# Sums over four tokens on VectorE or on TensorE, in the attention stage of a three-stage kernel

## The chip, the core and the metric

The kernel runs on one core of a Trainium2 chip. The metric is the device time of one execution in microseconds, as the median of three runs.

## The reference

Three layers follow each other. The first is attention over 4 batches, 8 heads, 576 tokens of 64 numbers, in two branches that are added: a coarse one, in which queries, keys and values are averaged over each four neighbouring tokens (144 positions), and a local one, in which each token sees the tokens less than four places away. The second is a layer of 8 experts with one expert a token, of which a linear score switches tokens off. The third is a gated layer of width 1536. Only the averages of queries and keys matter for the change.

```python
    q_d = q.reshape(B, H, Sd, factor, D).mean(axis=3)
    k_d = k.reshape(B, H, Sd, factor, D).mean(axis=3)
    v_d = v.reshape(B, H, Sd, factor, D).mean(axis=3)
    out_d = sm_attn(q_d, k_d, v_d)
    out_up = np.repeat(out_d, factor, axis=2)
...
    attn = attn / (np.sum(attn, axis=-1, keepdims=True) + 1e-09)
    out_local = np.matmul(attn, v)
    return (out_up + out_local).astype(np.float32)
```

## The kernel before

**The attention stage.** Queries and keys come in 12 units u of 192 tokens, three to a batch, and in each unit there are two loads n (0 queries, 1 keys) of 128 partitions (two heads of 64) by 4 head pairs by 192 tokens, in float32 (step `lq`, line 494, tile `qk`, five buffers). Float32 values are worked on as two float16 halves: ScalarE writes the high half (step `ph`, helper `hi_`, line 340) and VectorE subtracts it from the value for the low half (`pl`, helper `lo_`, line 343), both into the tile `qks` of the batch, of which there are two. The local branch (18 tiles i of 128 tokens: `ls` scores on TensorE, `lm` maximum and subtraction on VectorE, `le` exponential, `lt` and `lc` turn, `lV` values, `lr` and `ln` division) reads `qks`. The sums over four tokens (`pp`, line 511) are 16 products a unit: the float16 unit matrix times every fourth column of the halves, four columns and two halves accumulated in one PSUM bank for each of queries and keys (tile `qkd`). These sums are split into halves again, into the tile `qkh` (`qh` on ScalarE, `ql` on VectorE), and the coarse branch of a batch reads that (`ds` scores, line 548; `dm`, `dq`, `de`, `dt`, `dc`, `dv`, `dr`, `dn`) and writes its result to memory (`do`, tile `od`), from where each local tile loads its part (`lu`) and adds it (`xa`). GpSimd adds the coarse values of four tokens (`svd`, lines 539 and 540). The router follows (`gp`, `gd`, `gr`, `gk`), with GpSimd writing rows out by index.

**The order.** All steps of this stage are entered in a list with their engine, an estimated duration, the steps that they need, and the buffers that they take and release. A planner, class `Plan`, runs them through a model once, as the kernel is built: of the steps that are ready it takes the one that can start first, and of those the one with the least key, which is the length of the path behind it (negative) plus a correction from the table `PRI`. The instructions are then issued in that order on each engine's own in-order queue, and loads on SP's. Where the model sees TensorE without work for over 0.1 us, or with too few columns lately, it puts in filler products of zeros (line 411, 0.108 us in the model). Costs in the model: `pp` 1.6 us a unit on TensorE, `pl` 0.95, `ql` 0.54, `ls` 1.65, `lm` 1.7. The table `PRI` has 63 entries, one for each kind of step.

**After it** come the experts (first product at line 1060, in `h_first`), whose weights are loaded as buffers of the attention stage come free, and the gated layer.

## Time and profile before

| | us |
|---|---|
| median of 3 runs (747.73 to 748.56) | 748.16 |
| the profiled execution | 746.42 |
| its span, first to last instruction | 744.6 |
| TensorE / VectorE / ScalarE / GpSimd busy in the span | 704.0 / 498.7 / 386.7 / 282.6 |

The profiled execution is a single one; its span is the time from the first to the last instruction that the profiler recorded, and the rest of its time lies around that. Products are pipelined and their ends are modelled, so two that overlap count once in a busy time.

### The profile page before, as it was taken

The numbers are of one execution on the slowest core, as the hardware profiler recorded it, in microseconds if no ns is written. First come the engines' busy times: TensorE is split into PE (matmuls) and PEld (weight loads), VectorE is DVE, ScalarE is ACT, GpSimd is POOL, SyncE is SP. The second block draws the span as 40 slices with busy tenths as digits, with TensorE's granted clock in tenths as the row PEclk, the third lists the DMA queues.
The fourth block names the chain that finished last, engine by engine and source line by source line (L and its number), as shares of the span: only waits on it lengthen the run. The fifth ranks groups of instructions, "written<-read, shape, count | busy, mean of one in ns | idle before, by whom it ended". The sixth has DMA issues, their size and how long they took to land.

```text
span 744.6 us, 16389 instructions
## 1 busy us (share of the span) xinstructions
PE 704.0 (95%) x6567; PEld 466.7 (63%) x6567; DVE 498.7 (67%) x940; ACT 386.7 (52%) x766; POOL 282.6 (38%) x261
## 2 busy tenths in 40 slices
PE   8889788889899999989999899999999999999997
PEld 6677677778777888766665554455666666544443
DVE  6677587777688788769888989976668886300000
ACT  6565475452577776647777752445555655300000
POOL 5345575354100000236886775234434454200000
PEclk9999899999999999999999999999999999999999
DMA  8889887571799999865766511840000000001001
GB/s 258 246 267 273 190 208 197 149 176 50 230 353 341 346 364 284 269 218 183 217 179 187 155 27 42 163 92 1 2 0 1 1 1 1 1 28 43 29 29 42
DMA packets 95334, 108.82 MB, mean 146 GB/s; under 512 B 51248, under 2 KB 68658, under 8 KB 94679
## 3 DMA queue, kind: packets, MB, share of 16 engines
q1 hardware_dynamic: 91319, 99.80, 46.5%
q0 software_dynamic: 2880, 6.89, 2.9%
q10 hardware_dynamic: 1056, 1.05, 0.5%
q8 instruction: 52, 0.85, 0.5%
q14 instruction: 27, 0.22, 0.1%
HBM read 81.69 MB, written 17.30 MB: 133 GB/s over the span
## 4 chain that ended last, share of the span: by engine, by line
PE 42%; DVE 9%; ACT 3%; issue 3%; POOL 0%; ACTq 0%; DVEq 0%; POOLq 0%
PE p L1430 19%; PE op L1513 19%; PE gvp L1257 3%; DVE cb L1167 2%; DVE stg L1166 2%; DVE sg L1270 1%; DVE yg L1213 1%; DVE xphl L346 1%; ACT u L340 1%; ACT stg L1159 1%; ACT sg L1265 0%; DVE xpT L346 0%; ACT stg L1160 0%; PE xpp L1221 0%; ACT xpT L340 0%
## 5 line engine op out<-in xcount | busy, mean ns | idle before, releaser
L1513 PE MATMUL op<-w,u 128*128 128x512 f16 x648 | 140.2, 379 | 0.0
L1257 PE MATMUL gvp<-xpT,w 128*128 128x384 f16 (+1 forms) x720 | 111.1, 315 | 4.5 <-ACT sg L1265 2.2
L1513 PEld LDWEIGHTS <-u 128*128 128x128 f16 x648 | 63.5, 98 | 76.2
L1257 PEld LDWEIGHTS <-w 128*128 128x128 f16 x720 | 67.6, 98 | 47.2 <-issue 5.5
L343 DVE SCALAR_TENSOR_TENSOR w<-stg,w 128x1024 f16<-128x1024 f32 x64 | 79.7, 1273 | 17.9 <-ACT w L340 17.8
L346 POOL TENSOR_TENSOR w<-cb,w 128x512 f16<-128x512 f32 x36 | 52.2, 1450 | 83.6 <-ACT w L340 83.6
L1430 PEld LDWEIGHTS <-w 128*128 128x128 f16 x528 | 51.6, 98 | 36.1 <-issue 2.1
L340 ACT ACTIVATE w<-stg 128x1024 f16<-128x1024 f32 x64 | 65.7, 1051 | 16.0 <-DMA stg<-in_moe_w 14.6
L1048 PEld LDWEIGHTS <-w 128*128 128x128 f16 x672 | 55.7, 98 | 1.7
L1048 PE MATMUL hp<-xe,w 128*128 128x192 f16 x672 | 56.6, 246 | 0.0
L340 ACT ACTIVATE y<-op 128x512 f32<-128x512 f32 x18 | 10.7, 592 | 84.9 <-PE op L1513 84.4
L1430 PE MATMUL p<-t,w 128*128 128x384 f16 x244 | 50.1, 326 | 1.6 <-DVE sc L1303 1.6
L1430 PE MATMUL p<-xpT,w 128*128 128x384 f16 x264 | 46.5, 326 | 0.0
L1167 DVE SCALAR_TENSOR_TENSOR cb<-stg 128x512 int32<-128x512 int32 x36 | 42.1, 1171 | 3.5
L1430 PE MATMUL p<-t,s7h 128*128 128x384 f16 x176 | 42.9, 326 | 1.1 <-ACT sa L1454 1.1
L1083 PE MATMUL ya<-w,hT 128*128 128x512 f16 (+1 forms) x216 | 42.9, 356 | 0.0
L346 POOL TENSOR_TENSOR u<-sa,u 128x384 f16<-128x384 f32 x22 | 20.1, 915 | 49.9 <-ACT u L340 49.9
L1430 PEld LDWEIGHTS <-s7h 128*128 128x128 f16 x264 | 25.8, 98 | 18.3 <-issue 1.3
L511 PE MATMUL qkd<-qks,identh 128*128 128x192 f16 x192 | 34.7, 350 | 2.0 <-issue 2.0
L539 POOL TENSOR_TENSOR vr<-vr 72x1024 f32<-72x1024 f32 x8 | 18.8, 2356 | 41.7 <-DMA vr<-in_vr 38.4
L411 PE MATMUL wbank<-wz 128*128 128x252 bf16 x209 | 30.9, 287 | 2.5 <-POOL wz L407 1.3
L1083 PEld LDWEIGHTS <-hT 128*128 128x128 f16 x216 | 20.5, 98 | 20.3 <-issue 1.6
(196 smaller groups left out, 1389.8 us busy)
## 6 DMA issues: line engine op xcount, KB each, us to landing
stg<-in_moe_w SPq DMA_DIRECT2D x64, 512.0 KB
qk<-in_qk SPq DMA_DIRECT2D x24, 384.0 KB
stg<-in_moe_w_out SPq DMA_DIRECT2D x12, 512.0 KB
stg<-in_moe_w_gate SPq DMA_DIRECT2D x11, 512.0 KB
stg<-in_moe_w_val SPq DMA_DIRECT2D x11, 512.0 KB
vw<-in_vw SPq DMA_DIRECT2D x18, 284.4 KB
vr<-in_vr SPq DMA_DIRECT2D x8, 576.0 KB
up<-outd SPq DMA_DIRECT2D x18, 256.0 KB
```

The source lines that it names most:

```text
L340: act.activation(out=o, in_=i, func=func, scale=s)
L343: dve.scalar_tensor_tensor(out=o, in0=i, scalar=s, in1=h, op0=op, op1=ALU.subtract)
L346: eng.tensor_tensor(out=o, in0=i, in1=h, op=ALU.subtract)
L411: pe.matmul(out=wbank[:, 260:512], lhsT=wz[:, 0:128], rhs=wz[:, 0:252], start=True, stop=True)
L511: pe.matmul(out=p[:, n], lhsT=identh, rhs=qk_at(u, n, m // 4).rearrange("p b (g r) -> p b g r", r=4)[:, :, :, m % 4], start=(m == 0), stop ...
L539: pool.tensor_tensor(out=r[:, 0:2], in0=r[:, 0:2], in1=r[:, 2:4], op=ALU.add)
L1048: pe.matmul(out=p, lhsT=wt[e, kk][:, wl, m * 128:(m + 1) * 128], rhs=xe[e][:, xl + kk, :], start=(n == 0), stop=(n == 11))
L1083: pe.matmul(out=p, lhsT=hT[e][:, hl, m, 0:128], rhs=w[:, o:o + n], **f)
L1167: dve.scalar_tensor_tensor(out=b, in0=hi_w, scalar=3, in1=lo_w, op0=ALU.logical_shift_left, op1=ALU.bitwise_or)
L1257: pe.matmul(out=pp[n][:, o:o + width], lhsT=w[:, wl, n, kk * 128:(kk + 1) * 128], rhs=xpT[blk][:, xl + kk, o:o + width], start=(j == 0), s ...
L1430: pe.matmul(out=p, lhsT=l(wl)[:, 128 * kk:128 * kk + 128], rhs=rr(xl, kk), start=first and j == 0, stop=last and j == 5, skip_group_check= ...
L1513: pe.matmul(out=p, lhsT=u[:, ul, t * 128:(t + 1) * 128], rhs=w[:, wl, f % 2, :], start=(n == 0), stop=(n == 3 * NF - 1))
```

## The change

The sums are made by VectorE, by one reduction for each loaded tile (two a unit), straight from the float32 tile `qk` into a float32 tile `qkd` in SBUF, of which there are two. The step `pp` thereby becomes two steps, `("pp", u, 0)` and `("pp", u, 1)`, on VectorE's queue at 0.88 us each in the plan; they need the load alone and release the loaded tile, which now has three readers. The tile `qks` loses three readers a batch, and the sums take no PSUM bank. Since the float32 values are not scaled yet, the splitting of the sums (`qh`, `ql`) scales them. The planner's key gets a second correction, for a single step, and the table `PRI` has 904 entries, 841 of them for single steps, with other values for the kinds too. The entry of `pp` in the table of columns that count for TensorE's fillers goes. The two tables are cut here.

```diff
--- before.py
+++ after.py
@@ -53,7 +53,7 @@
 C_IO = C_MASK + 4 * W
 C_N = C_IO + CAP
 
-PRI = {'cs': -192.4, 'ct': 204.9, 'dc': -158.3, 'de': 83.2, 'dm': -115.1,
...
+PRI = {'cs': 29.0, 'ct': 151.8, 'dc': 13.5, 'de': 89.5, 'dm': -179.4,
...
+        ('pp', 5, 0): 58.5, ('pp', 5, 1): 16.6, ('lv', 5): -22.6, ('lm', 7): -20.2, ('lt', 8, 0): -41.4,
...
 
 
 def constants():
@@ -136,7 +136,7 @@
             return t
 
         kind = lambda n: n[0] if isinstance(n, tuple) else n
-        key = {n: (ops[n][6] + self.pri.get(kind(n), 0.0) - length(n), m) for m, n in enumerate(ops)}
+        key = {n: (ops[n][6] + self.pri.get(kind(n), 0.0) + (self.pri.get(n, 0.0) if isinstance(n, tuple) else 0.0) - length(n), m) for m, n in enumerate(ops)}
         ready = [n for n in ops if not nneed[n]]
         base = {n: 0.0 for n in ready}
         order, when, busy, lock = [], {}, [], {}
@@ -504,12 +504,10 @@
                     qks[b] = a2.tile([128, 2, 2, 4, S], F16, tag="qks", name="qks")
                 hi_(qk_at(u, n, 0), qk[u, n], SQ)
 
-            def prep_p(u):
-                p = qkd[u] = bank([128, 2, 4, 48], "qkd")
-                for n in range(2):
-                    for m in range(8):
-                        pe.matmul(out=p[:, n], lhsT=identh, rhs=qk_at(u, n, m // 4).rearrange("p b (g r) -> p b g r", r=4)[:, :, :, m % 4],
-                                  start=(m == 0), stop=(m == 7), skip_group_check=True)
+            def prep_p(u, n):
+                if n == 0:
+                    qkd[u] = a2.tile([128, 2, 4, 48], F32, tag="qkd", name="qkd")
+                dve.tensor_reduce(out=qkd[u][:, n].rearrange("p b (g o) -> p b g o", o=1), in_=qk[u, n].rearrange("p b (g r) -> p b g r", r=4), axis=AX.X, op=ALU.add)
 
             def prep_l(u, n):
                 lo_(qk_at(u, n, 1), qk[u, n], qk_at(u, n, 0), SQ)
@@ -521,10 +519,10 @@
             def pool_h(u):
                 if u // 3 not in qkh:
                     qkh[u // 3] = a2.tile([128, 2, 2, 4, S // 4], F16, tag="qkh", name="qkh")
-                hi_(qkh_at(u, 0), qkd[u], 1.0)
+                hi_(qkh_at(u, 0), qkd[u], SQ)
 
             def pool_l(u):
-                lo_(qkh_at(u, 1), qkd[u], qkh_at(u, 0), 1.0)
+                lo_(qkh_at(u, 1), qkd[u], qkh_at(u, 0), SQ)
 
 
             vr, dS, dP, dTp, dT, dO, dR, od = {}, {}, {}, {}, {}, {}, {}, {}
@@ -863,7 +861,7 @@
                 scat.append(d.ins)
 
 
-            pl = Plan({"bank": 7, "fb": 1, "qk": NQK, "qks": 2, "qkh": 2, "vw": NV, "vr": 1, "vd": 2, "dP": 2, "dT": 2,
+            pl = Plan({"qkd": 2, "bank": 7, "fb": 1, "qk": NQK, "qks": 2, "qkh": 2, "vw": NV, "vr": 1, "vd": 2, "dP": 2, "dT": 2,
                        "od": 1, "lP": 2, "lT": 3, "xhl": 6, "up": 2, "xT": 2, "stg": NST, "lr": 3, "dr": 3}, PRI)
             DL = 2.0
             tiles_of = {b: [i for i in range(NTILE) if b in ((2 * i) // 9, (2 * i + 1) // 9)] for b in range(B)}
@@ -882,14 +880,15 @@
                 for n in range(2):
                     z = (u, n)
                     first = u % 3 == 0 and n == 0
-                    pl.add(("lq",) + z, "SP", 1.2, lambda z=z: load_qk(*z), take=[("qk", ("qk",) + z, 2)], late=DL)
+                    pl.add(("lq",) + z, "SP", 1.2, lambda z=z: load_qk(*z), take=[("qk", ("qk",) + z, 3)], late=DL)
                     pl.add(("ph",) + z, "ACT", 0.82, lambda z=z: prep_h(*z), need=[("lq",) + z] + ([] if first else [("ph", 3 * b, 0)]), rel=[("qk",) + z],
-                           take=[("qks", ("qks", b), len(tiles_of[b]) + 3)] if first else [])
+                           take=[("qks", ("qks", b), len(tiles_of[b]))] if first else [])
                     pl.add(("pl",) + z, "DVE", 0.95, lambda z=z: prep_l(*z), need=[("ph",) + z], rel=[("qk",) + z])
-                pl.add(("pp", u), "PE", 1.6, lambda u=u: prep_p(u), need=["ih", ("pl", u, 0), ("pl", u, 1)], take=[("bank", ("pb", u), 1)], rel=[("qks", b)])
-                pl.add(("qh", u), "ACT", 0.49, lambda u=u: pool_h(u), need=[("pp", u)] + ([("qh", 3 * b)] if u % 3 else []),
+                for n in range(2):
+                    pl.add(("pp", u, n), "DVE", 0.88, lambda u=u, n=n: prep_p(u, n), need=[("lq", u, n)] + ([("pp", u, 0)] if n else []), take=[] if n else [("qkd", ("qkd", u), 1)], rel=[("qk", u, n)])
+                pl.add(("qh", u), "ACT", 0.49, lambda u=u: pool_h(u), need=[("pp", u, 1)] + ([("qh", 3 * b)] if u % 3 else []),
                        take=[] if u % 3 else [("qkh", ("qkh", b), 4)])
-                pl.add(("ql", u), "DVE", 0.54, lambda u=u: pool_l(u), need=[("qh", u)], rel=[("pb", u)])
+                pl.add(("ql", u), "DVE", 0.54, lambda u=u: pool_l(u), need=[("qh", u)], rel=[("qkd", u)])
             for b in range(B):
                 for c in range(2):
                     pl.add(("lvd", b, c), "SP", 2.2, lambda b=b, c=c: load_vd(b, c), take=[("vr", ("vr", b, c), 1)], late=DL)
@@ -995,7 +994,7 @@
             ms = tc.manual_schedule()
             ms.__enter__()
             pl.run({"PE": 1.2, "POOL": 1.0}, fill, "PE", 0.108, 0.1, 252.0,
-                   {"pp": (3072.0, 3072.0), "ls": (2240.0, 2240.0), "lt": (0.0, 1024.0), "lV": (1040.0, 1040.0), "ds": (864.0, 864.0), "dt": (0.0, 648.0),
+                   {"ls": (2240.0, 2240.0), "lt": (0.0, 1024.0), "lV": (1040.0, 1040.0), "ds": (864.0, 864.0), "dt": (0.0, 648.0),
                     "om": (4608.0, 4608.0), "oe": (1536.0, 1536.0), "dv": (2080.0, 2080.0), "xp": (0.0, 1024.0)}, 3.41, LEAST, 10.24 / 3, 3200.0)
             ms.__exit__(None, None, None)
```

## Rows read from the trace of the kernel before

**Rows 1.** The page: busy time and share by engine; DMA share by slice.
```profile
PE 704.0 (95%) x6567; PEld 466.7 (63%) x6567; DVE 498.7 (67%) x940; ACT 386.7 (52%) x766; POOL 282.6 (38%) x261
...
DMA  8889887571799999865766511840000000001001
```

**Rows 2.** Timeline, the stage's end: start, us, engine, line, operation, [idle before].
```profile
189.89 4.23 SPq L364 DMA_DIRECT2D stg<-in_moe_w  x3
...
190.46 2.73 PE L1060 MATMUL hp<-xe,w 128*128 128x192 f16 x31 [0.65 <-DVE xe L853]
```

**Rows 3.** Stretches, all engines: from:to, length, then as the first line says.
```profile
core 0: us, PE busy (x) PEld busy (x) DVE busy (x) ACT busy (x) POOL busy (x), PEclk, DMA share, GB/s
5.90:120.00 114.10, 99.74 (x1640) 78.74 (x1640) 84.17 (x197) 68.48 (x149) 61.97 (x48) 0.96 0.87 238
120.00:176.00 56.00, 49.79 (x1055) 42.25 (x1055) 43.70 (x168) 28.63 (x65) 25.64 (x23) 1.00 0.56 148
176.00:190.50 14.50, 12.87 (x145) 11.48 (x143) 8.24 (x47) 3.00 (x7) 7.06 (x7) 1.00 0.24 70
...
40.00:60.00 20.00, 17.99 (x390) 15.02 (x389) 15.88 (x40) 15.09 (x37) 7.85 (x4) 1.00 0.86 269
100.00:113.00 13.00, 10.78 (x125) 8.38 (x121) 13.00 (x20) 8.12 (x13) 12.13 (x8) 0.87 0.85 215
```

**Rows 4.** The same for line 511, the sums' products, alone.
```profile
10.00:116.00 106.00, 33.49 (x186) 20.52 (x184) 0.95 0.87 237
```

**Rows 5.** The same for line 411, the filler products, alone.
```profile
10.00:116.00 106.00, 3.68 (x18) 1.71 (x18) 0.95 0.87 237
```

**Rows 6.** Timelines of single engines: the coarse branch of the last batch.
```profile
94.21 0.65 PE L631 MATMUL sl<-qks 64*64 64x70 f16 x48
...
99.14 3.03 ACT L340 ACTIVATE qks<-qk 128x768 f16<-128x768 f32 x4
...
103.88 2.92 PE L511 MATMUL qkd<-qks,identh 128*128 128x192 f16 x16 [1.99 <-issue]
...
107.41 0.84 ACT L340 ACTIVATE qks<-qk 128x768 f16<-128x768 f32 x1 [1.00 <-DMA qk<-in_qk]
...
113.09 2.92 PE L511 MATMUL qkd<-qks,identh 128*128 128x192 f16 x16
...
118.97 0.55 DVE L343 SCALAR_TENSOR_TENSOR qkh<-qkd,qkh 128x384 f16<-128x384 f32 x1
...
119.57 0.86 PE L548 MATMUL sd<-qkh 64*72 64x144 f16 x12 [1.53 <-DVE qkh L343]
...
147.11 0.31 SPq L609 DMA_DIRECT2D outd<-od  x1
```

**Rows 7.** Lines by form, 0 to 195 us: count | busy us, mean ns | idle before.
```profile
L343 DVE SCALAR_TENSOR_TENSOR qks<-qk,qks 128x768 f16<-128x768 f32 x24 | 28.7, 1207 | 3.1 <-ACT qks L340 3.1
...
L641 DVE TENSOR_REDUCE lmx<-sl 128x4 f32<-128x280 f32 x36 | 14.3, 438 | 4.2 <-PE sl L631 4.1
...
L343 DVE SCALAR_TENSOR_TENSOR qkh<-qkd,qkh 128x384 f16<-128x384 f32 x12 | 6.5, 546 | 2.5 <-ACT qkh L340 2.5
```

**Rows 8.** Timeline: GpSimd and VectorE instructions beside each other.
```profile
60.40 2.36 POOL L539 TENSOR_TENSOR vr<-vr 72x1024 f32<-72x1024 f32 x1 [5.52 <-DMA vr<-in_vr]
...
60.66 2.92 DVE L343 SCALAR_TENSOR_TENSOR qks<-qk,qks 128x768 f16<-128x768 f32 x1
...
166.64 1.16 POOL L346 TENSOR_TENSOR xhl<-x,xhl 128x512 f16<-128x512 f32 x1 [2.91 <-ACT xhl L340]
...
166.69 0.17 DVE L764 TENSOR_REDUCE gef<-geq 128x3 f32<-128x24 f32 x1
...
166.89 0.93 DVE L765 TENSOR_TENSOR gef<-gef,gpen 128x3 f32<-128x3 f32 x1
```

**Rows 9.** Line 343, 0 to 192 us: count, shortest/median/longest ns, first and last start.
```profile
L343 DVE SCALAR_TENSOR_TENSOR qks<-qk,qks x24: 942/958/3058, 5.9 to 110.1; 128x768 f16<-128x768 f32 x24
L343 DVE SCALAR_TENSOR_TENSOR qkh<-qkd,qkh x12: 540/545/558, 12.9 to 119.0; 128x384 f16<-128x384 f32 x12
```

2 lines of the change are left out of this document (1 added, 1 removed).

## The prediction, made before the changed kernel was run

> **What bounds the kernel now.** I read the page first: TensorE is busy for 95% of the span and VectorE for 67%, and the 16 DMA engines are nearly full in the first third [rows 1]. These shares are averages over several stages, and the edit touches one, the attention stage, so the second view was a table of stretches. The stage ends where the first expert product starts, at 190.46 us; the expert weights' loads go out 0.57 us before that [rows 2]. All that follows hangs on that instant, since the buffers for the further weights and TensorE's own queue are released there: I take a shift of 190.46 to move the end of the kernel by as much. Nothing behind it is edited.
>
> Inside the stage the table says this [rows 3]. From 5.9 us (VectorE's first subtraction) to 120 us TensorE is busy 99.74 of 114.1 us, the DMA engines 0.87, VectorE 84.17. From 120 to 176 VectorE has 43.70 of 56. From 176 on there is a serial tail of the last router groups, with VectorE at 8.24 of 14.5. So TensorE is the fullest engine of the first part, and of its work from 10 to 116 us the sums over four tokens are 33.49 us [rows 4]: 186 recorded products (of 192), 0.18 us each. Filler products, which the plan puts in wherever it believes TensorE idle, are only 3.68 us there [rows 5]. The plan counts one of the 12 sum steps (16 products) as 1.6 us; 16 x 0.18 is 2.9. So TensorE runs later than its plan by 1.3 us for each.
>
> The third view was the timeline along the last batch's coarse branch [rows 6], the longest path I could follow by hand. The last local tile of batch 1 is multiplied at 94.21, which frees the buffer of halves; the conversions of batch 3 then start at 99.14, the last one at 107.41, right when its transfer lands (1.00 us of waiting for the DMA). The sums of batch 3 run on TensorE from 103.88 to 116.0, in three pieces with other work between; the last subtraction of the sums is at 118.97, the first coarse scores at 119.57, and the coarse result is written out at 147.11, after which the last tiles can load it.
>
> **What it removes.** 192 products, 33.5 us of TensorE by [rows 4], and one of seven PSUM banks for each of the 12 units. It is not a gain by itself: TensorE's order is made from the plan, and what the plan saw as 12 x 1.6 = 19.2 us of work it may fill with filler products of 0.108 us, some 178 of them. By [rows 5] a filler costs 3.68/18 = 0.20 us standing alone, so 178 are at most 36 us: the time that TensorE is given back lies between 33.5 and about nothing. I count nothing for it directly, and take its value from the chain instead.
>
> **What moves.** The sum no longer waits for the conversion (ScalarE), the subtraction (VectorE) and the buffer of halves; it waits for its load and VectorE. For batch 3 the last input is there at 107.41 [rows 6]. Add one sum (0.9, below), the conversion of the sums (about 0.5) and their subtraction (0.55, [rows 7]): 109.4, against 119.57. The coarse branch of the last batch can start 10.2 us earlier without any load being earlier. Against it, each loaded tile is now held by three readers, not two, and there are five such buffers; a sum that stands late in VectorE's queue delays the next load on SP's queue, and behind that load stand the value windows and the up-loads. I take nothing for it, since the sum needs no more than the subtraction that already holds the buffer; where it ran last it would cost the 0.9 us of one sum.
>
> **What it adds.** 24 reductions of 128x768 float32 on VectorE. The trace has none of that size. The 128x280 reductions take 438 ns [rows 7], one over 24 elements 0.17 us [rows 8]: 1.05 ns an element, so 0.438 + 488 x 0.00105 = 0.95. Busy time per instruction, in which overlapping ends count once, gives 14.3/36 = 0.40 and by the same steps 0.83. The subtraction of the same 768 elements has a median of 0.958 [rows 9]. I take 0.9: 21.6 us, bounds 19.9 and 23.
>
> The second added cost is hidden in an unchanged line: the subtraction of the sums (12 of them) now reads its 384 numbers from SBUF instead of PSUM. From PSUM it takes 540 to 558 ns always; the subtraction on loaded tiles, both inputs in SBUF, goes from 942 to 3058 [rows 9]. One of these, 2.92 us at 60.66, stands beside GpSimd's addition at 60.40, and at 166.64 GpSimd subtracts while a two-input VectorE operation at 166.89 takes 0.93 for three numbers; the reduction just before it, at 166.69, takes its usual 0.17 [rows 8]. So the moved subtractions can be stretched and the new reductions, by that one row, not. Mean over median of the 24 is 1.207 - 0.958 = 0.25 us; 12 x 0.25 = 3.0 us. Bounds are 0 (GpSimd quiet at each) and 12 x 2.1 = 25 (the longest stretch each time); the mean is nearest, being the same operation in the same stage. The Trainium skill's page "SBUF — State Buffer", section "Who interferes with whom", has the same in general: on this chip a reduction never contends with GpSimd, an instruction with two SBUF inputs does with a GpSimd instruction that reads SBUF. By that rule 0 goes on the 24 reductions, which the row at 166.69 bears out, and 0 to 25 on the 12 subtractions.
>
> **The sum.** VectorE's dense stretch, 5.9 to 176, is 84.17 + 43.70 = 127.9 us of work in 170.1. It becomes 127.9 + 21.6 + 3.0 = 152.5. If the stage kept its length VectorE would be at 89.7% there; if it took the 10.2 us of the chain, at 95.4%. VectorE replaces TensorE as the engine that sets the pace, and the question is how full its in-order queue can be. Two dense stretches of the trace, 40 to 60 and 100 to 113, hold 28.88 of 33 us, 87.5%; the second alone is 100% [rows 3]. I take the middle, 93.75%: the first of the two held waits on work that the old plan priced at half, while the 0.88 us with which the new plan prices a sum agrees with the 0.9 from the rows; but nothing shows that a whole stage packs like 13 us of it. 152.5/0.9375 = 162.7, which is 7.4 us less than 170.1. The profiled execution took 746.42 us (span 744.6): 739.0. The median of the three runs is 748.16, 1.74 above: **741**.
>
> **Rivals.** First, VectorE fills but does not pack: at the 87.5% of those two stretches the 152.5 us need 174.3, that is +4.2 us, 752. It decides from 89.7% downward. For it speaks that GpSimd's work already stretches VectorE [rows 8], and that a queue in order can't pass a sum whose load is late (the loads come at 0.87 of the DMA engines). Against it, that much of VectorE's idle time now was waiting for TensorE. The Trainium skill's page "VectorE: DVE Perf Modes", section "Rules for kernel authors", calls the reduction the slowest VectorE operation and advises to restructure it away; by that rule this rival holds. No run here has a reduction of this size yet.
>
> Second, no change: the transfers pace the first 120 us (0.87 busy, [rows 3]), the batches' buffers still turn at the local tiles' pace, fillers take the place of the products, and the stage ends where it did: 747 to 750. Against it, after 120 us the share falls to 0.56, and the order there is VectorE's and TensorE's to set.
>
> Third, more than I forecast: the branch's 10.2 us come through whole, and the new order packs the second part too (VectorE is only at 78% from 120 to 176). With VectorE at 100% the stretch would be 152.5, or 17.6 less: 730.6. That is the floor, and between it and 736 lies this case.
>
> The granted clock stands at 0.96 from 5.9 to 120 us and at 1.00 after; with TensorE emptier it could be lower in places. I put this into the first and second rival: TensorE has up to 33 us to give before that counts.
>
> **Chances.** Forecast (736 to 746): 0.55. More: 0.17. No change, within 0.2%, which is about what a measurement of this kernel can tell from none (1.5 us): 0.08. Slower: 0.20. So faster 0.72, same 0.08, slower 0.20. The range goes from the floor, 731, to the first rival with its one microsecond of rounding and profile spread, 753; the forecast's own is 736 to 746.
>
> **What would show it.** Right: no products on the sums' line, 24 reductions of 0.83 to 0.95 us that do not stretch beside GpSimd, the last batch's first coarse scores near 109 us rather than 119.6, VectorE at 92% or more of the stretch to 176, the first expert product near 183, and the stages behind it unchanged in length. Wrong: a reduction well over 1 us, the moved subtractions at 1 us or more each, VectorE at 88% with waits on loads or on TensorE's fillers between, or a first expert product at 190 or later. A changed length of the expert stage would break the step that shifts the end one for one.

## The result: slower, not faster

| | changed | before, same runs | ratio, 95% interval |
|---|---|---|---|
| first timing | 757.06 us (749.58 to 762.95, 19 runs) | 748.16 | 1.0094 [1.0074, 1.0114] |
| repeat (e13) | 750.77 us (747.95 to 756.44, 12 runs) | 748.93 | 1.0043 [1.0010, 1.0077] |

The ratios leave out slow runs (four of the 19, over 1.5% above the kernel's fastest) and are not quotients of the medians. 741 was forecast, with 731 to 753 as the range. The change is slower by 0.4 to 0.9%: the first rival's side. The two intervals barely touch (1.0074 to 1.0077), and each ratio lies outside the other's interval, so the size is less certain than either says, and an edit of the changed kernel is read only against the kernel before in its own timing. Differences of half a per cent between edits from different timings are not used.

The first profile of the changed kernel is of an execution of 757.2 us, the repeat's of one of 747.95, the shortest of its twelve. The page of the first, busy time, beside [rows 1]:

```profile
PE 709.7 (94%) x6619; PEld 474.6 (63%) x6619; DVE 516.2 (68%) x964; ACT 386.2 (51%) x766; POOL 280.9 (37%) x261
```

VectorE has gone from 498.7 to 516.2 us. Stretches of it, columns as in [rows 3]; the last one ends at the first expert product, now at 202.3:

```profile
5.90:120.00 114.10, 96.87 (x1748) 80.86 (x1745) 97.14 (x219) 69.22 (x151) 59.90 (x47) 0.91 0.89 236
120.00:176.00 56.00, 46.73 (x882) 38.19 (x878) 39.98 (x145) 25.08 (x58) 21.57 (x19) 0.88 0.57 150
176.00:202.30 26.30, 22.76 (x262) 19.85 (x259) 15.95 (x72) 5.65 (x12) 12.17 (x11) 1.00 0.16 46
```

The same of the repeat, whose first expert product is at 194.34:

```profile
5.90:120.00 114.10, 96.84 (x1749) 80.54 (x1747) 97.92 (x219) 69.44 (x151) 58.89 (x48) 0.94 0.87 236
120.00:176.00 56.00, 48.09 (x965) 40.43 (x966) 44.45 (x158) 27.28 (x62) 25.14 (x21) 0.97 0.54 150
176.00:194.30 18.30, 16.31 (x172) 14.18 (x170) 11.72 (x59) 3.83 (x9) 9.38 (x9) 1.00 0.22 66
```

VectorE's work in the stage is 153.1 and 154.1 us, where [rows 3] add up to 136.1. It fills 80.6% and 83.7% of the stretch from 5.9 to 176, where it filled 75.2. So most of the time that was added is there, and the packing that the forecast needed is not. VectorE's queue can be fuller than that: with every sum issued twice (e2 below) the same stretch holds 154.5 us of its work, 90.8%. The lines by cost, columns as in [rows 7]:

```profile
L411 PE MATMUL wbank<-wz 128*128 128x252 bf16 x453 | 67.9, 294 | 11.5 <-DVE od L603 9.0 <-POOL wz L407 1.3 <-DVE drc L596 0.7
...
L343 DVE SCALAR_TENSOR_TENSOR qks<-qk,qks 128x768 f16<-128x768 f32 x24 | 23.5, 987 | 0.0
...
L510 DVE TENSOR_REDUCE qkd<-qk 128x192 f32<-128x768 f32 x24 | 22.3, 946 | 7.1 <-DMA qk<-in_qk 7.1
...
L343 DVE SCALAR_TENSOR_TENSOR qkh<-qkd,qkh 128x384 f16<-128x384 f32 x12 | 9.3, 777 | 0.0
```

The reductions take 0.946 us, as forecast, and the subtraction of the sums has gone from 546 to 777 ns (860 in the repeat), near the forecast. What the forecast lacked lies beside them: the subtraction of the loaded tiles was stretched less, 987 ns and not 1207, and fillers went from 209 to 453.

The last batch's coarse branch, in single engines' timelines, answers to [rows 6]:

```profile
109.47 0.95 DVE L343 SCALAR_TENSOR_TENSOR qks<-qk,qks 128x768 f16<-128x768 f32 x1
...
110.44 0.36 SPq L494 DMA_DIRECT2D qk<-in_qk  x1
...
113.68 0.95 DVE L510 TENSOR_REDUCE qkd<-qk 128x192 f32<-128x768 f32 x1 [0.35 <-DMA qk<-in_qk]
...
116.48 1.62 DVE L343 SCALAR_TENSOR_TENSOR qkh<-qkd,qkh 128x384 f16<-128x384 f32 x1
...
118.25 0.57 PE L546 MATMUL sd<-qkh 64*72 64x144 f16 x12
...
132.13 0.56 PE L546 MATMUL sd<-qkh 64*72 64x144 f16 x12
...
154.70 0.33 SPq L607 DMA_DIRECT2D outd<-od  x1
...
202.29 3.07 PE L1059 MATMUL hp<-xe,w 128*128 128x192 f16 x24 [2.29 <-DVE xe L851]
```

And of the kernel before, where [rows 6] don't have them:

```profile
99.04 2.10 DVE L795 SCALAR_TENSOR_TENSOR gso<-gpen,gso 128x4 f32<-128x4 f32 x1
...
101.06 0.95 DVE L343 SCALAR_TENSOR_TENSOR qks<-qk,qks 128x768 f16<-128x768 f32 x1
...
102.04 0.35 SPq L494 DMA_DIRECT2D qk<-in_qk  x1
...
126.94 0.57 PE L548 MATMUL sd<-qkh 64*72 64x144 f16 x12
```

The last load is issued right behind a subtraction of a loaded tile in both, 0.02 to 0.03 us after its end, but at 110.44 and not at 102.04: 8.4 us later. From its issue to the first coarse scores it now takes 7.81 us, where [rows 6] with the issue at 102.04 give 17.53, so the chain behind the load is 9.7 us shorter. Of this, 2.1 us is the transfer (3.2 us from issue to landing, not 5.4). From landing to scores it takes 4.6 us, where it took 12.2 and the forecast had 2.0: between the sum and the subtraction of the sums stand 1.85 us in which VectorE works on local tiles and waits for TensorE, where 0.5 us of conversion was counted, and that subtraction takes 1.62 us. The coarse branch itself, from first scores to the write-out, takes 36.45 us and not 27.54: its third group of score products starts 13.9 us after the first, in the kernel before 7.4. The new order also puts off the last subtractions of loaded tiles, the 24th to 139.2 us, where [rows 9] have 110.1. Sum by sections, to the first expert product: +8.40 - 9.72 + 8.91 + 4.24 = +11.83 in the first profile, and +8.37 - 10.17 + 6.62 - 0.94 = +3.88 in the repeat's.

### The profile page after: what moved, and what is told of

Read it like the earlier page. It is cut to its first block, busy times and chain, and to the rows that moved or that the text cites. A ratio compares the mean times of both kernels' runs of the same rounds, so it can differ in the third digit from the quotient of the medians.

```text
span 755.4 us, 16480 instructions
## 1 busy us (share of the span) xinstructions
PE 709.7 (94%) x6619; PEld 474.6 (63%) x6619; DVE 516.2 (68%) x964; ACT 386.2 (51%) x766; POOL 280.9 (37%) x261
## 4 chain that ended last, share of the span: by engine, by line
PE 41%; DVE 8%; ACT 3%; issue 3%; POOL 0%; ACTq 0%; DVEq 0%; POOLq 0%
PE p L1429 19%; PE op L1512 19%; PE gvp L1256 3%; DVE cb L1166 2%; DVE stg L1165 2%; DVE sg L1269 1%; DVE yg L1212 1%; DVE xphl L346 1%; ACT u L340 1%; ACT stg L1158 1%; ACT sg L1264 0%; DVE xpT L346 0%; ACT stg L1159 0%; PE xpp L1220 0%; ACT xpT L340 0%
## 5 line engine op out<-in xcount | busy, mean ns | idle before, releaser
L411 PE MATMUL wbank<-wz 128*128 128x252 bf16 x453 | 67.9, 294 | 11.5 <-DVE od L603 9.0
L411 PEld LDWEIGHTS <-wz 128*128 128x128 bf16 x453 | 46.1, 106 | 18.6 <-issue 9.5
L346 POOL TENSOR_TENSOR xhl<-x,xhl 128x512 f16<-128x512 f32 x18 | 22.6, 1259 | 25.9 <-ACT xhl L340 25.8
```

Source lines behind the costliest of these rows:

```text
L346: eng.tensor_tensor(out=o, in0=i, in1=h, op=ALU.subtract)
L411: pe.matmul(out=wbank[:, 260:512], lhsT=wz[:, 0:128], rhs=wz[:, 0:252], start=True, stop=True)
```

## Two places of loss in the trace

GpSimd, VectorE and TensorE of the first profile at 54 us:

```profile
53.84 2.34 POOL L537 TENSOR_TENSOR vr<-vr 72x1024 f32<-72x1024 f32 x1 [5.72 <-PE sl L629]
...
53.85 2.35 DVE L558 TENSOR_SCALAR dmx<-dmx 72x4 f32<-72x4 f32 x1
59.35 0.95 DVE L510 TENSOR_REDUCE qkd<-qk 128x192 f32<-128x768 f32 x1 [3.15 <-DMA qk<-in_qk]
60.22 0.41 DVE L603 TENSOR_TENSOR od<-wbank,drc 72x256 f32<-72x256 f32 x1
...
54.30 0.60 PE L652 MATMUL tl<-cs,lP 128*70 128x128 f32 x4
60.68 1.00 PE L411 MATMUL wbank<-wz 128*128 128x252 bf16 x4 [5.79 <-DVE od L603]
```

VectorE's operation on four numbers (in each of 72 partitions) is held for 2.35 us, as long as GpSimd's addition; then the sum at the head of VectorE's queue waits 3.15 us for its load, with the copy `od` behind it; TensorE's filler waits for `od`, since `wbank` holds d_v's output too, and loses 5.79 us. The granted clock from 60 to 70 us is 0.66 afterwards, against 1.00 before. The repeat's rows:

```profile
57.59 0.95 DVE L510 TENSOR_REDUCE qkd<-qk 128x192 f32<-128x768 f32 x1 [4.30 <-DMA qk<-in_qk]
...
58.92 1.00 PE L411 MATMUL wbank<-wz 128*128 128x252 bf16 x4 [4.76 <-DVE od L603]
```

So this stall comes back. The other place does not: in the first profile everything slows at 164 to 168 us, where there are no sums,

```profile
167.83 0.17 PE L742 MATMUL lg<-w,xT 128*128 128x9 f16 x1 [0.57 <-issue]
...
166.40 0.45 DVE L639 TENSOR_REDUCE lmx<-sl 128x4 f32<-128x280 f32 x1 [2.26 <-PE tl L652]
...
167.87 0.60 ACT L340 ACTIVATE xT<-xpp 128x512 f16<-128x512 f32 x1 [4.85 <-remote]
```

and the granted clock falls to 0.70 from 170 to 180 us. The repeat has none of it (clock 1.00). From the last local scores to the first expert product the first profile takes 39.4 us, the repeat 33.2, the kernel before 30.2 (from 160.22). These 6.2 us are most of the 7.95 us by which the first expert products of the two profiles differ. Why three engines waited together there stays open; ScalarE's wait is for something the profile doesn't name.

## The experiments

Theory 1: VectorE's time for the sums paces the stage. Theory 2: the sums' place does, as they wait at the head of its queue. Theory 3: fillers and TensorE's clock. Theory 4: the new order. Each ratio is to the kernel before in the same timing. The last columns are instants of the one profile of each, a single execution that can lie far from the median (e6's took 746.98 us, the shortest of its twelve): the last load's issue, the last batch's first coarse scores, the first expert product.

| run | us | ratio, interval | load | scores | product |
|---|---|---|---|---|---|
| before | | | 102.04 | 119.57 | 190.46 |
| e1 quarter | 748.64 | 1.0010 [0.9975, 1.0045] | 109.08 | 116.32 | 193.97 |
| e2 twice | 766.86 | 1.0249 [1.0211, 1.0288] | 122.91 | 131.25 | 204.17 |
| e3 no late fill | 748.12 | 0.9998 [0.9971, 1.0025] | 114.27 | 121.85 | 195.70 |
| e4 old table | 762.51 | 1.0192 [1.0157, 1.0228] | 123.23 | 134.95 | 208.77 |
| e5 before, no late fill | 754.26 | 1.0109 [1.0067, 1.0150] | 108.21 | 123.31 | 198.59 |
| e6 before, few products | 752.59 | 1.0067 [1.0034, 1.0100] | 102.47 | 118.14 | 190.82 |
| e7 before, sums added | 755.31 | 1.0116 [1.0082, 1.0151] | 113.40 | 129.44 | 200.14 |
| e8 quarter, no late fill | 752.33 | 1.0065 [1.0039, 1.0091] | 109.54 | 117.03 | 195.94 |
| e9 tiny sums | 749.00 | 1.0011 [0.9982, 1.0040] | 110.58 | 117.82 | 195.01 |
| e10 constant | 749.80 | 1.0031 [1.0011, 1.0052] | 109.01 | 116.25 | 193.75 |
| e11 third of fill | 748.42 | 0.9993 [0.9963, 1.0022] | 108.71 | 115.76 | 192.15 |
| e12 before, replaced | 751.21 | 1.0036 [1.0004, 1.0068] | 104.90 | 122.39 | 196.25 |
| e13 changed again | 750.77 | 1.0043 [1.0010, 1.0077] | 110.41 | 117.77 | 194.34 |
| e14 tail fill only | 750.22 | 1.0025 [0.9995, 1.0056] | 111.59 | 119.17 | 194.59 |
| e15 early fill only | 747.75 | 0.9999 [0.9969, 1.0030] | 108.95 | 116.20 | 194.76 |
| e16 wait and constant | 753.35 | 1.0055 [1.0027, 1.0084] | 111.75 | 119.11 | 196.25 |
| e17 last batch | 757.86 | 1.0144 [1.0113, 1.0174] | 106.60 | 121.57 | 199.38 |
| e18 three batches | 754.20 | 1.0075 [1.0047, 1.0103] | 108.20 | 121.95 | 199.34 |

**How long a sum takes (e1, e2, e9).** The edits, each to the sums' line of the changed kernel:

```diff
 # e1: the input is cut
+in_=qk[u, n].rearrange("p b (g r) -> p b g r", r=4)[:, :, :, 0:1]
 # e2
+for _ in range(2):
+    dve.tensor_reduce(...)
 # e9: 4 outputs into a standing tile
+dve.tensor_reduce(out=qkd[u][:, n, 0:1, 0:1]..., in_=qk[u, n][:, 0:1, 0:4]...)
```

> The changed kernel in its own order, but each of the 24 sums reads only the first token of every four (192 numbers in place of 768; the output leaves out three quarters of every sum over four tokens). Theory 1, VectorE's time: the sums add some 22 us to the engine that orders the stage, and that time reaches the end. A sum should fall from 0.95 us to between 0.25 and 0.45 us, which frees 12 to 17 us of VectorE, and the time should fall by 7 us or more, from 757 to 750 or lower. Theory 2, the place of the sums: a sum that heads VectorE's queue before its load has landed stops all that is queued behind it, however short the sum is; the waits for loads (7.1 us) and the stall at 54 to 60 us stay, and the time falls by less than 4 us. Theory 3, the fillers and the clock of TensorE: unchanged here, so less than 4 us as well.

> The changed kernel in its own order, with every sum issued twice in a row (24 more reductions of some 0.9 us, 22 us more of VectorE; the result is the same). Theory 1: VectorE's time paces the stage, so most of the 22 us shows: 757 becomes 772 to 780. Theory 2: what the sums cost is where they wait, and the second sum never waits for a load; part of the added time falls into idle time of VectorE (15 to 29 per cent of the stage): 757 becomes 759 to 768. Theory 3: under 765.

> The changed kernel in its own order, with each sum cut to 4 of its 192 outputs (the others keep a constant, so the output leaves out nearly all sums). The instruction, its place in the queue and its wait for the load stay; its time should fall from 0.95 us to about 0.1, some 20 us of VectorE in all. Theory 1: the price rises with VectorE's time (a sum of 0.50 us gave back 8.4 us, of 1.9 us cost 9.8 more), so the time falls below the 748.6 us of the quarter, to 739 to 745, and the new order would be worth several us if the sums were free. Theory 2 (place, waits and the order cost, and not the time): 746 to 750, no better than the quarter.

The sums' lines of e1 and e2, and the sums of e9 by shortest/median/longest ns:

```profile
L510 DVE TENSOR_REDUCE qkd<-qk 128x192 f32<-128x192 f32 x24 | 11.7, 502 | 11.9 <-DMA qk<-in_qk 11.9
```

```profile
L511 DVE TENSOR_REDUCE qkd<-qk 128x192 f32<-128x768 f32 x48 | 45.1, 948 | 1.1 <-DMA qk<-in_qk 0.3
```

```profile
L512 DVE TENSOR_REDUCE qkz<-qk x24: 138/150/157, 5.2 to 113.7; 128x1 f32<-128x4 f32 x24
```

The 24 sums take 3.6, 12.0 (as counts times means), 22.7 and 45.5 us, and the kernel costs +0.11, +0.10, +0.43 to +0.94, and +2.49%. Up to 12 us cost nothing that can be told; the last 22.8 cost 1.55 to 2.06%, 11.6 to 15.4 us. Theory 1 holds in this form only: VectorE has slack, and past it half to two thirds of each microsecond shows; e2's 766.86 lies in the range that theory 2 had named, 759 to 768. That the changed kernel's own 22.7 us cost anything is clear against the first timing alone, since the intervals of e1 and e9 overlap the repeat's. And e9 refutes what theory 1 promised for free sums, 739 to 745: the new order is then no faster than the kernel before. Its rows show one reason, VectorE's and SyncE's:

```profile
109.61 0.95 DVE L343 SCALAR_TENSOR_TENSOR qks<-qk,qks 128x768 f16<-128x768 f32 x1
...
110.58 0.36 SPq L497 DMA_DIRECT2D qk<-in_qk  x1
...
113.73 0.16 DVE L512 TENSOR_REDUCE qkz<-qk 128x1 f32<-128x4 f32 x1 [0.26 <-DMA qk<-in_qk]
```

With a sum of 0.16 us the subtraction that frees the last buffer still stands at 109.61, and in e10 below, where the sums read no loaded tile, the load still goes out at 109.01. So in the new order neither the sums' time alone nor their hold on the buffers alone makes the load late; what is left is the order, with that instruction's place in it. No run has both away. The longer coarse branch is the order's too: from first scores to write-out it takes 35.7 us here (to 153.56), and with the changed code in the old order (e4) 27.2 (134.95 to 162.15).

**Where a sum waits (e10, e16).**

```diff
 # e10: the same size out of a constant tile
-in_=qk[u, n].rearrange("p b (g r) -> p b g r", r=4)
+in_=qz.rearrange("p b (g r) -> p b g r", r=4).to_broadcast([128, 4, 48, 4])
 # e16: e10 with the reduction of e9 in front of it
```

> The changed kernel in its own order, with the same 24 reductions reading a constant tile in place of the loaded one (the output leaves out the sums). VectorE's time stays (24 times 0.95 us); a sum no longer waits for a load (7.1 us in the changed kernel) and no longer holds one of the five load buffers. Theory 2, waiting and holding: the last load of queries and keys is issued near 102 us again and not at 110.4, the last batch's first coarse scores come before 113 us, and the time falls by 5 us or more, to 752 or lower. Theory 1: VectorE reaches the same work as late as before, and the time stays within 3 us of 757.

> The changed kernel in its own order, with each sum replaced by two reductions: one of 4 outputs out of the loaded tile, which waits for the load as the sum did, and one of the full size out of a constant tile (the output leaves out the sums; 2 to 4 us more of VectorE than the changed kernel). Short sums that wait gave 749.0, long sums that don't wait 749.8, long ones that wait 757. Theory 2, waiting and working together use up VectorE's slack: 755 to 761 here. If it stays under 752, neither the wait nor the time is the cause, and the changed kernel's loss comes from something else that an edit of the sums alters.

e10's own expectation by theory 2 failed in two of three: the last load is issued at 109.01, and the scores come at 116.25. e16's 753.35 lies between the two ranges of its expectation. e10's time, +0.31%, and e16's, +0.55%, lie on either side of the repeat's +0.43%, and all three intervals overlap. The waits at the head of the queue are seen in the trace (7.1 and 7.0 us in the two profiles); what they are worth is under what these runs can tell, and theory 2 stays unsettled.

**Fillers (e3, e5, e8, e11, e14, e15).** One edit, with other bounds each time (e5 in the kernel before with 32; e8 together with e1's):

```diff
 def fill():
+    nfill[0] += 1
+    if nfill[0] <= 69:   # e11: or nfill[0] % 3 == 0; e14: not 69 < nfill[0] <= 300; e15: <= 300
         pe.matmul(out=wbank[:, 260:512], ...)
```

> The changed kernel in its own order without the 384 filler products that stand after the start (453 become 69; the fillers compute nothing that is used). Theory 3a, fillers hold up TensorE: they share a tile with d_v's output and wait for VectorE's copy of it (9.0 us), and they stand in front of real products; without them the time falls by 4 us or more, to 753 or lower. Theory 3b, fillers hold up the clock: without them the granted clock in the stage, 0.66 to 0.99 in stretches of 10 us, falls further, real products take longer, and the time rises by 5 us or more, to 762 or higher. Theories 1 and 2: TensorE is not what sets the stage's end, and the time stays within 4 us of 757.

> The kernel before in its own order, without the 177 filler products that stand after the start (209 become 32). If fillers as such cost time (theory 3a taken for both kernels), this falls below 748 by about 177/384 of the 9 us that the changed kernel gained by losing 384 of them: some 4 us, to 744. If fillers cost only where the order has them stand in the way, as in the changed kernel, the time stays within 2 us of 748. If they earn their place by the clock, it rises by 3 us or more, to 751 or higher.

> The changed kernel in its own order with both cuts: the sums read a quarter of their numbers (output leaves out the rest) and the 384 later fillers are gone. Each cut alone gave 8 to 9 us. If they are two causes, they add: 757 becomes 738 to 742. If they are two ends of one chain (VectorE's late copies hold the fillers, the fillers hold the products that VectorE waits for), the second cut finds little: 745 to 749.

> The changed kernel in its own order with the start's 69 fillers and every third one after it (197 in place of 453, near the 209 of the kernel before). Dropping all 384 gave 9 us. If the fillers' own time on TensorE is what costs, two thirds of it come back: about 751. If some fillers earn by the clock and others only stand in the way, this lies below both ends: 742 to 747, faster than the kernel before. If the gain came from a few places where a filler waits for VectorE's copy out of the shared tile, it lies between 748 and 757 with no clear rule.

> The changed kernel in its own order without the 231 fillers numbered 70 to 300 (those between the start and some 158 us); the 153 of the tail stay. If the fillers of the dense part, between VectorE's late copies and the products, cost the 9 us, the time falls to 747 to 750; if those of the tail cost it, it stays at 754 to 758.

> The changed kernel in its own order without the 153 fillers from number 301 on (those after some 158 us); the earlier 300 stay. If the fillers of the tail cost the 9 us (their queue in front of the router's products), the time falls to 747 to 750; if those of the dense part cost it, it stays at 755 or rises, since nothing then holds TensorE's clock up in the tail.

In the kernel before the 177 late fillers are worth 1.1%: without them the granted clock from 5.9 to 120 us is 0.88 and not 0.96. Whether the clock makes the difference is not shown; e5's profile also has a late load, which is taken up under e17. In the changed kernel 384 are worth nothing that can be told (e3, e11, e15 stand at the kernel before's time, at or a little under the changed kernel's), though the clock in that stretch is 0.78 in e3 and 0.91 and 0.94 in the changed kernel. That the fillers take back in TensorE's queue what they hold up of the clock would fit, but is not shown. e8's 752.33 lies in neither range of its expectation; with short sums fillers may be worth something again (e8 against e1, two timings). The expectations of 4 to 9 us from single groups were made against 757 and fall with it. One pair belongs to a single timing: the twelve times of e15, without the tail's fillers, have a mean of 748.3 us and the repeat's one of 751.6, so 3.3 us less, with an interval of 0.8 to 5.8. As the largest of three such differences (e14, e15, e16) it is a hint that the tail's fillers cost something, no more.

**The order (e4).** The changed code with the 63 keys of the old table.

> The changed kernel's operations put in order with the table of the kernel before (63 keys by kind, none by single operation). Theory 4, the new order itself loses the time: the time comes to 748 or lower. Theory 1: VectorE's work is the same in either order, so the stage ends near 202 us or later: 754 to 775, since this table was not made for the sums. Theory 2: the sums stand elsewhere in VectorE's queue; the time goes with the time that VectorE waits for loads with a sum at its head (7.1 us in the changed kernel), one for one.

+1.9%: the last load goes out at 123.23. Theory 4, that the new keys lose the time, is refuted; this code is about a per cent faster with them. Theory 2's one for one fails as well: VectorE waits 4.3 us for loads at a sum here, less than the 7.1 us of the changed kernel, and the time is longer.

**The two halves of the edit in the old order (e6, e7, e12).**

```diff
 # e6: with start and stop in that one
-for m in range(8):
+for m in range(1):
 # e7: behind the subtraction of each load
+dve.tensor_reduce(out=qkx[u][:, n]..., in_=qk[u, n]..., axis=AX.X, op=ALU.add)
 # e12: seven of eight
+pe.matmul(out=p[:, n], lhsT=wz[:, 0:128], rhs=wz[:, 0:192]..., start=True, stop=True)
```

> The kernel before in its own order, with 1 of each 8 products that make the sums (24 of 192 matmuls left, so the sums are not the reference's). This is the removal alone, some 30 us of TensorE with nothing put in its place. By the prediction's step (TensorE's products are worth nothing in themselves) the time stays within 3 us of 748. If TensorE paced the stage, it falls by 8 us or more, to 740 or lower. If the products' activity held TensorE's clock up, the granted clock of the stage falls under 0.95 and the time rises by 3 us or more.

> The kernel before in its own order, with the 24 reductions added behind each subtraction of the split, into a tile that nothing reads (24 times 0.95 us, 22.8 us more of VectorE; TensorE's products stay). A reduction here never waits for a load. Theory 1, VectorE's time paces the stage: between half and all of it shows, 748 becomes 759 to 771. Theory 2, the place of the sums matters and not their time: within 5 us, under 753.

> The kernel before in its own order, with 7 of each 8 products of the sums replaced by products of the zero tile, of the same columns, into the same bank (the output leaves out seven eighths of each sum). Dropping the products without a replacement cost 5 us, 748 to 752.6, with a granted clock of 0.52 to 0.67 from 10 to 40 us. If that loss was the clock's, the clock stays over 0.8 from 10 to 40 us here and the time is within 2 us of 748. If the loss came otherwise (an order that fits worse without the products), the time stays at 751 or higher.

Taking the products away, alone, makes the kernel 0.7% slower. Stretches of e6's profile, columns as in [rows 3]; the kernel before has a clock of 1.00 in all three:

```profile
10.00:20.00 10.00, 3.79 (x60) 2.51 (x60) 6.65 (x12) 5.52 (x10) 0.94 (x2) 0.67 0.97 266
20.00:30.00 10.00, 7.92 (x100) 5.22 (x99) 9.05 (x20) 7.49 (x19) 3.62 (x2) 0.65 0.62 182
30.00:40.00 10.00, 7.54 (x84) 6.53 (x86) 3.94 (x14) 3.73 (x12) 3.60 (x2) 0.52 0.96 252
```

And of e12, with zero products in their place:

```profile
10.00:20.00 10.00, 7.96 (x165) 6.94 (x156) 7.32 (x12) 5.08 (x8) 0.94 (x2) 1.00 0.96 267
20.00:30.00 10.00, 7.52 (x119) 5.39 (x117) 9.87 (x21) 8.04 (x21) 3.61 (x2) 1.00 0.65 213
30.00:40.00 10.00, 6.99 (x97) 6.12 (x97) 3.82 (x12) 3.30 (x10) 3.60 (x2) 0.83 0.96 243
```

The clock is back, the time is not: 751.21 lies on the side that the expectation gave to another cause, an order that fits worse without the products. And the execution of e6 whose low clock is shown above (0.78 from 5.9 to 120 us) took 746.98 us and had the first expert product at 190.82, 0.36 us later than before. All twelve executions of e6 have a mean clock of 0.950 to 0.969 (the kernel before in that timing 0.982 to 0.993), and they take 747.0 to 759.9 us. So a lower clock comes with the products' removal, but in some executions it costs nothing, and why e6 is slower on the whole stays open. Adding the sums alone costs 1.2% (755.31, between the ranges of the two theories): the last load is issued 11.4 us later, the first expert product comes 9.7 later.

**The changed kernel once more (e13).** No edit.

> The changed kernel once more, for a second profile and a second interval. In its first profile 5.8 us of TensorE are lost at 54 to 61 us (a filler waits for VectorE's copy, and a sum had waited 3.15 us for its load in front of that copy), and from the last local scores (162.9 us) to the first expert product (202.3) it takes 39.4 us, where five edited versions take 31 to 33. Theory 2, the chain of waits: the time is again 755 to 759, and the stall near 54 to 61 us is there again. If the long tail is a chance of one execution, it takes 31 to 34 us in this profile; if it belongs to the kernel, 37 us or more.

+0.43%. The stall at 54 to 60 us came back, the long tail did not, and 750.77 misses theory 2's 755 to 759.

**The predicted chain by itself (e17, e18).** Old order, the sum in front of each subtraction for the last batch only, or for the last three.

```diff
 def prep_p(u):
+    if u >= VS:          # 9 in e17, 3 in e18
+        return
 def prep_l(u, n):
+    if u >= VS:
+        dve.tensor_reduce(out=qkd[u][:, n]..., in_=qk[u, n]..., axis=AX.X, op=ALU.add)
     lo_(qk_at(u, n, 1), qk[u, n], qk_at(u, n, 0), SQ)
 # and the splitting of these sums scales them, as in the change
```

> The kernel before in its own order, with the last batch's sums alone made by VectorE (6 reductions, each in front of the subtraction of its load; 48 of the 192 products are gone; the reference's result). This is the prediction's chain by itself: 5.7 us of VectorE and 8.7 us of TensorE less, with the last batch's products at 103.9 to 116.0 us out of the way. By the prediction's step the first coarse scores of that batch move from 119.6 to 111 to 115 us and the stage's end moves with them one for one: 741 to 745. If the end doesn't hang on that branch (by the same or another chain it is the local tiles or the transfers that end last), the scores move and the time stays at 747 to 750. If VectorE's queue takes it back (a weight subtraction of 3.5 us stands before the last subtraction of sums), the scores stay near 119.

> The kernel before in its own order, with the sums of three of the four batches made by VectorE (18 reductions, 17 us; 144 of 192 products gone; the reference's result): three quarters of the change without its new order. Adding all 24 sums to the kernel before cost 7.7 us, dropping its products 5.0. If the two prices add, three quarters of 12.7 us, some 9: 756 to 759, and the new order of the changed kernel is worth several us. If the shorter chain of the last batch pays for part of it: 749 to 754. If the changed kernel's loss is its new order, this is at 748 or lower.

The clearest failure: six sums, with 48 products fewer, cost 1.4%. GpSimd, VectorE, TensorE and SyncE of e17:

```profile
99.72 1.27 POOL L546 TENSOR_TENSOR vd<-vr 72x512 f32<-72x512 f32 x1
100.94 1.26 POOL L698 TENSOR_TENSOR x<-x,up 128x512 f32<-128x512 f32 x1
102.16 2.26 POOL L346 TENSOR_TENSOR xhl<-x,xhl 128x512 f16<-128x512 f32 x2
...
99.92 4.53 DVE L800 SCALAR_TENSOR_TENSOR gpen<-rk,gpen 128x4 f32<-128x4 f32 x1
104.37 0.41 DVE L611 TENSOR_TENSOR od<-wbank,drc 72x256 f32<-72x256 f32 x1
...
104.77 0.94 DVE L520 TENSOR_REDUCE qkd<-qk 128x192 f32<-128x768 f32 x1
105.63 0.94 DVE L343 SCALAR_TENSOR_TENSOR qks<-qk,qks 128x768 f16<-128x768 f32 x1
...
104.83 2.18 PE L598 MATMUL wbank<-vd,dT 128*72 128x65 f32 x16 [4.97 <-DVE od L611]
...
106.60 0.35 SPq L494 DMA_DIRECT2D qk<-in_qk  x1
...
121.57 0.33 PE L554 MATMUL sd<-qkh 64*72 64x144 f16 x2
```

One VectorE operation, of the router, is held beside GpSimd's until 104.45; behind it wait `od`, for which TensorE idles 4.97 us, and a sum and the subtraction that frees the last buffer, so the last load goes out at 106.60, 4.56 us later than before. But this hold begins before the first of the six sums, at 104.77. The sum itself puts 0.86 us in front of the load; the other 3.7 us are the hold. In the kernel before the router's longest operation there is the one of 2.10 us at 99.04, and e5, where VectorE has no sums at all, shows the long one too:

```profile
102.36 4.55 DVE L798 SCALAR_TENSOR_TENSOR gpen<-rk,gpen 128x4 f32<-128x4 f32 x1
...
107.24 0.94 DVE L343 SCALAR_TENSOR_TENSOR qks<-qk,qks 128x768 f16<-128x768 f32 x1
...
108.21 0.35 SPq L498 DMA_DIRECT2D qk<-in_qk  x1
```

Of the profiles of the kernel before and its edits, e5, e7, e17 and e18 have a router operation of 4.53 to 4.55 us in this place and the last load 4.6 to 11.4 us late; the kernel before, e6 and e12 have none over 2.20 us, and in e6 and e12 the load is 0.4 and 2.9 us late. So in this order the load hangs on how these small operations meet GpSimd's more than on the sums; in e7 they also come 6.1 us later. One profile of each can't say how often it falls so.

e18 fits this: 18 sums cost 0.75%, less than e17's six, in the same timing and with intervals that don't meet, so the price doesn't go with the number of sums. Its 754.20 lies just above the second range of its expectation.

In e17 VectorE is busy without a gap from 100 to 120 us. The scores come at 121.57, later than the 119.57 they were to beat, and with the last batch's products gone the granted clock from 100 to 130 us is 0.66, 0.60 and 0.71 (before: 0.83, 1.00, 1.00). That both happen is shown; the share of each is not. The first product's +8.9 us agrees with the time.

## Why the prediction was wrong

- **What it adds** was right: 24 sums at 0.946 us (0.9 taken), not stretched; the moved subtractions +0.23 us each, +0.31 in the repeat (0.25 taken). The sum of 24.6 us became 17 to 18 in the stage, in good part because the loaded tiles' subtraction was stretched less, by 5.2 and 3.9 us. The Trainium skill's rule for the reduction, in "VectorE: DVE Perf Modes", section "Rules for kernel authors", that it is the slowest operation, is not what the trace shows for these float32 tiles: it costs what the subtraction of the same tile does when undisturbed (0.942).
- **What moves** is the step that failed: "The coarse branch of the last batch can start 10.2 us earlier without any load being earlier", with nothing taken for a later load "since the sum needs no more than the subtraction that already holds the buffer". From the load's landing on the chain did shorten, by 7.6 and 8.0 us; not all of what it had been was the removed steps, for 2.2 us of it were VectorE's queue, with a weight subtraction of 3.53 us (115.52) in front of the last subtraction of sums. But the subtraction that frees the last buffer stands in VectorE's queue, and the load left 0.02 to 0.03 us after it in the kernel before (102.04), both profiles of the changed kernel, e9 and e17. In the new order that subtraction came 8.4 us later, and about as late with tiny sums (e9). So the scores came 1.3 to 1.8 us earlier and not 10.2. The branch from there to its write-out, which the prediction's sum left as it was, grew by 8.9 and 6.6 us, and by that alone the coarse result was later than before. In the old order one sum puts 0.86 us in front of the load (e17), the "0.9 us of one sum" that the prediction allowed; the rest of e17's delay is a router operation beside GpSimd, a stretch that the prediction had seen in its row at 166.89 and counted for the moved subtractions alone.
- **The sum**: the packing of 93.75% was not reached (80.6 and 83.7%). The first rival, at 87.5% with 752, named waits behind late loads and GpSimd, which the traces have, and its break-even of 89.7% was the right side; that its 752 lies so near is in part luck, since VectorE was less full than it said. That VectorE "replaces TensorE as the engine that sets the pace" is not borne out at this size: in e9 VectorE has 127.8 us of work from 5.9 to 176, as much as before the change, and the first expert product still comes at 195.01.
- **What it removes**: "I count nothing for it directly" holds in that no run shows a gain; e6 puts the removal at +0.7% in the old order. The step "TensorE has up to 33 us to give before that counts" is not settled: the products did keep the clock up, but e6's profiled execution went without that at no cost.
- **One for one**: the first expert product at +3.88 and +11.83 us went with spans of +1.5 and +10.8, so the stages behind give back 1 to 2.4 us. Nearly right.
- No experiment beats the kernel before (the lowest ratio, e11's 0.9993, is a tie), and with the sums' price nearly gone (e9) there is no gain either: in this order the change had none for that price to eat.

## What to carry to other kernels

Before counting on work that can start earlier, follow the instruction that releases the load buffer, and what stands in front of it in its queue, and not only the one that uses the buffer: here a new order made the last load late with hardly any work added (e9), and in the old order small operations beside GpSimd did most of it without any (e5). Before counting removed work as free, ask what it did for TensorE's clock; but a low clock in one stretch is not yet a loss (e6). And time a kernel twice when half a per cent matters.

## What the runs showed of the hardware

- A VectorE operation on four numbers can take 4.53 us. In e17 it began at 99.92 beside GpSimd's addition and ended at 104.45, as the fourth GpSimd instruction from 99.72 on ended (102.16 + 2.26 = 104.42, two instructions), so it was held through all that followed. The same four GpSimd instructions and a VectorE operation of 4.53 to 4.55 us that ends with the last of them stand in the profiles of e5, e7 and e18. The Trainium skill's page "SBUF — State Buffer", section "Who interferes with whom", says that whichever engine has the shared ports holds them for its whole instruction; the row at 53.85 agrees with one instruction, and e17 shows that the wait can go over several.
- Products of 192 columns whose moving operand takes every fourth number follow each other in 0.177 us (32 in 5.67 us from 15.60 on, before), products of 192 columns side by side in 0.083 (seven in 0.58 us from 10.38 to 10.96, e12), both at a granted clock of 1.00. They differ in type and weights too, float16 and bfloat16 zeros, so that the step between the numbers is the cause is likely, not shown.
- The same kernel, timed twice, gave 1.0094 [1.0074, 1.0114] and 1.0043 [1.0010, 1.0077], each ratio outside the other's interval.
